# A seven-product form for the second MLP's output product, two blocks of tokens at a time

## The chip, the cores and the metric

The kernel runs on one NeuronCore of one Trainium2 chip. The metric is the device time of one execution in microseconds. Five engines have their own instruction queues: TensorE (PE in the profile; its weight loads are PEld), VectorE (DVE), ScalarE (ACT), GpSimd (POOL) and SyncE (SP), which here issues all DMAs.

## The reference, cut to what matters

```
attn = local attention over chunks of 32 tokens, with 8 memory slots   # 4 x 8 heads x 768 x 64
x = attn as 3072 tokens x 512
h = max(x @ w1, x @ w2, x @ w3)          # d_ff 768
y = h @ w_mid                            # 3072 x 512 (called moe_w_out)
u = y @ w_in                             # 512 -> 2048
g = u if u >= 1;  0 if u <= -1;  (u + 1)**2 / 4 between
out = g @ w_out                          # 2048 -> 512
```

The weights are float64 in memory, q, k, v and the memory float32, and so is the output.

## The kernel before, in words

Tokens are worked on in 6 blocks of 512 (`TB`), features in tiles of 128 (`P`). Every product is made of float32 operands that are split in a rounded high part (`hi`, type fp32r) and the rest (`lo`); `mm3` (L495) then issues three matmuls: hi x hi, hi x lo, lo x hi. A split is a ScalarE copy that writes `hi` and a subtraction on GpSimd or VectorE that writes `lo`.

Three stages follow one another. Up to about 450 us, the attention of later blocks runs interleaved with the first MLP (`slot_l1`, `slot_l2`) of earlier blocks; the order is a list written out by hand (`PLAN`, for block 0), and then a loop over `order` with one attention step for each slot. In its gaps the float64 weights of the second MLP are rounded (`round_step`: `abs_w`, `tail_w`, `bits_w`, `sum_w`), first 8 pairs of w_out tiles and then 8 pairs of w_in tiles, one pair in six slots, and stored to DRAM: w_out to `wd`, w_in to `cd` together with four sums of its quarters (`combine_w`). Then comes the first MLP of the last block, some 63 us, in which `LAST_BLOCK` names what else is done at each slot: the blocks' y is loaded and its sums made (`prep`), and w_out comes back from `wd` and is split (`w_step`, `split_w`).

From about 519 us the second MLP runs for three pairs of blocks. Its product with w_in is in the seven-product form already: the two halves of d_model and the two blocks of a pair are the quarters of one matrix, w_in's quarters those of the other. `pair_slot` (L662) makes the seven products of one n (eight n for a pair), adds them from the PSUM banks to the four result tiles (VectorE, L679 to L712) and applies the activation (`g_relu` on ScalarE, `g_rest` on VectorE). Between its products `mid` puts the product with w_out of the pair's first block (`slot_l4`, L724); the second block's runs after the pair's last n, 14 or 16 steps in a row. `slot_l4` is the ordinary product: for each of 16 tiles f of d_ff, four groups of 128 tokens, three matmuls each with 128 tokens of h stationary and 512 columns of w_out moving. For each f of a block, h is split once (`split`, ScalarE L513 and GpSimd L515). `split_c` splits a 256-wide w_in operand for a coming product (ScalarE L585, GpSimd L586). `NEXT_PAIR` names the steps at which `prep` of the next pair runs: loads of y's quarters A to D, differences T1 to T4 (L636, L639), and seven splits (L616, L617).

Each engine works through its queue in the order in which the program issues. A buffer tag with a number of `bufs` is a ring: a new tile of the tag waits until the oldest one's readers are done.

Of the kernel before, what the change touches and what calls it, by code (L numbers as in the profile page):

```python
# [65 lines left out]
def attention_then_two_mlps(ctx, tc, q, k, v, mem_k, mem_v, w1, w2, w3, w_mid, w_in, w_out, out):  # L66
# [38 lines left out]
    round2 = [("d", f) for f in range(K2)] + [("c", f + h) for f in range(HF) for h in (0, HF)]  # L105
# [45 lines left out]

    def combine_w(st, c):
# [33 lines left out]

    def load_w(q):
        n = 2 * (q - Q1)
        staged[q] = stage.tile([P, 2, TB], F32, tag="st", name=f"w{q}", bufs=2)
        nc.sync.dma_start(out=staged[q], in_=wd[n:n + 2].rearrange("t p f -> p t f"))  # L190

    def split_w(q, pool):
        new_w(q, pool)
        t = staged.pop(q)
        hi, lo = split2.pop(q)
        nc.scalar.copy(out=hi, in_=t)
        nc.vector.tensor_tensor(out=lo, in0=t, in1=hi.bitcast(F32), op=ALU.subtract)

# [344 lines left out]
    def slot_l2(j, f):  # L543
        hi, lo = hs.pop(("A", j, f))
        whi, wlo = weights["b", f]
        for d in range(KD):
            c = slice(d * P, (d + 1) * P)
            mm3(acc[d], whi[:, c], wlo[:, c], hi, lo, f == 0, f == K1 - 1)
            if f == K1 - 1:
                y = mx.tile([P, TB], F32, tag=("hh", "hl")[d % 2], name=f"y_{j}_{d}", bufs=3)  # L550
# [7 lines left out]
    OPERANDS = "b11 b21 b22 t1 t2 t3 t4".split()  # L558
    PRODUCTS = [(0, "b11"), (2, "t2"), (1, "b21"), (3, "t3"), (4, "t1"), (5, "t4"), (6, "b22")]
    PARTS = 4  # L560
    mat, raw, cs, late, keep = {}, {}, {}, {}, []
    total = NB // 2 * HF * 7
    put, loaded, limit = [0], [0], [HF * 7]

# [13 lines left out]
    def split_c():  # L578
# [5 lines left out]
        cs[s] = c = rp.tile([P, 2, HK], F32R, tag="cr", name=f"cs{s}", bufs=8)  # L584
# [22 lines left out]
    def halves_of(y):  # L607
        return [y[:, i] for i in range(2)] if not isinstance(y, list) else y

    def split_y(name, y):  # L610
        if name not in mat:
            mat[name] = new_mat(name)
        t = mat[name]
        for hi, lo, x in zip(halves_of(t[:, 0]), halves_of(t[:, 1]), halves_of(y)) if isinstance(y, list) else (
                (t[:, 0], t[:, 1], y),):
# [3 lines left out]
    def prep(p):  # L619

        v = {}

        def load(name, j, h):
            v[name] = y = stage.tile([P, 2, TB], F32, tag="c", name=f"{name}_{p}", bufs=2)
            nc.sync.dma_start(
                out=y, in_=yd[2 * h * P:2 * (h + 1) * P, j * TB:(j + 1) * TB].rearrange("(k p) t -> p k t", p=P))

        def load2(name, j, h):
            v[name] = [rp.tile([P, TB], F32, tag="cr", name=f"{name}{i}_{p}", bufs=8) for i in range(2)]
            for i in range(2):  # L630
                r = (2 * h + i) * P
                nc.sync.dma_start(out=v[name][i], in_=yd[r:r + P, j * TB:(j + 1) * TB])

        def sub(out, a, b):
            if not isinstance(v[a], list) and not isinstance(v[b], list):
                nc.vector.tensor_tensor(out=v[out], in0=v[a], in1=v[b], op=ALU.subtract)  # L636
                return
            for o, x, y in zip(*[halves_of(v[n]) for n in (out, a, b)]):
                nc.vector.tensor_tensor(out=o, in0=x, in1=y, op=ALU.subtract)  # L639

        return {
            "A": lambda: load("A", 2 * p, 0), "C": lambda: load("C", 2 * p + 1, 1),
            "B": lambda: load2("B", 2 * p + 1, 0), "D": lambda: load2("D", 2 * p, 1),
            "b11": lambda: split_y("b11", v["A"]), "b22": lambda: split_y("b22", v["C"]),
            "b21": lambda: split_y("b21", v["D"]),
            "T1": lambda: sub("B", "B", "A"), "T2": lambda: sub("C", "C", "B"),
            "T3": lambda: sub("A", "C", "A"), "T4": lambda: sub("D", "D", "C"),
            "t1": lambda: split_y("t1", v["B"]), "t2": lambda: split_y("t2", v["C"]),
            "t3": lambda: split_y("t3", v["A"]), "t4": lambda: split_y("t4", v["D"]),
        }  # L650

    def g_relu(x, a):
# [3 lines left out]
    def g_rest(x, a):  # L656
        nc.vector.scalar_tensor_tensor(out=a, in0=a, scalar=1.0, in1=x, op0=ALU.min, op1=ALU.max)

    def kept_h(f):
        return keep[f // 2][:, f % 2]  # L660

    def pair_slot(p, n, mid):  # L662

        s, j = (p * HF + n) * 7, 2 * p
        V = nc.vector
        add = partial(V.tensor_tensor, op=ALU.add)

        def next_product(k):
            bank = banks[4 + (s + k) % 4]
# [4 lines left out]
        c11 = mx.tile([P, TB], F32, tag="y", name=f"c11_{s}", bufs=2)  # L674
        nc.scalar.copy(out=c11, in_=b)
        split_c()
        b = next_product(1)
        c12 = mx.tile([P, TB], F32, tag="y", name=f"c12_{s}", bufs=2)
        add(out=c12, in0=b, in1=c11)  # L679
        split_c()  # L680
        mid(0)
        b = next_product(2)
        add(out=c11, in0=b, in1=c11)  # L683
        a11 = mx.tile([P, TB], F32, tag="t", name=f"a11_{s}", bufs=2)
        g_relu(c11, a11)
# [12 lines left out]
        split(("B", j, n), a11, f"b{j}_{n}")
        split_c()
        mid(1)  # L700
        g_rest(c22, h22)
        b = next_product(5)
        add(out=c21, in0=b, in1=c21)
        a21 = mx.tile([P, TB], F32, tag="t", name=f"a21_{s}", bufs=2)
        g_relu(c21, a21)
        split_c()
        if n == HF - 1:
            g_rest(c21, a21)
            split(("B", j, n + HF), a21, f"b{j}_{n + HF}")
            mid(2)  # L710
        b = next_product(6)
        add(out=c12, in0=b, in1=c12)  # L712
        h12 = kept_h(n)
        g_relu(c12, h12)
        if n < HF - 1:
            g_rest(c21, a21)
            split(("B", j, n + HF), a21, f"b{j}_{n + HF}")
            split_c()
            mid(2)
        else:  # L720
            split_c()
        g_rest(c12, h12)

    def slot_l4(i, f):  # L724
        hi, lo = hs.pop(("B", i, f))
        whi, wlo = weights["d", f]
        first, last = f == 0, f == K2 - 1
        for t in range(TB // P):
            c = slice(t * P, (t + 1) * P)
# [257 lines left out]
```

## Time and profile before

| | us |
|---|---|
| three runs | 1023.65, 1025.57, 1026.11 |
| median | 1025.57 |
| the profiled execution | 1025.52 |
| its span, first to last instruction | 1023.7 |

The profile is of one execution. Busy time of an engine is the time in which at least one of its instructions runs; a matmul's duration includes its way through the pipeline, so durations of neighbours overlap. The page and the answers give times in us from the start of the span, unless marked ns.

### The profile page before, as it was taken

The page shows a single profiled execution, that of the slowest core. Times are in us where ns is not written, and L with a number is a line of the kernel's source. Part 1 is how long each engine was busy: PE and PEld are TensorE (multiplying, and loading weights), DVE is VectorE, ACT ScalarE, POOL GpSimd, SP SyncE. Part 2 cuts the span into 40 slices and gives each one's busy share as a digit, 9 for nine tenths or more (in the row PEclk, how much of TensorE's full clock was granted, in tenths as well). Part 3 has the DMA queues.
Part 4 walks back from the last instruction along what each step waited for, and adds up shares of the span by engine and source line. Part 5 has one row for each costly group of instructions (what it writes and reads, how often), then busy time and mean ns, then how long its engine had stood idle before and what let it go on. Part 6 is the DMA issues. An engine that isn't in the chain of part 4 may idle for free.

```text
span 1023.7 us, 18842 instructions
## 1 busy us (share of the span) xinstructions
PE 1001.3 (98%) x7398; PEld 807.6 (79%) x7398; DVE 560.5 (55%) x880; ACT 473.7 (46%) x835; POOL 331.5 (32%) x316
## 2 busy tenths in 40 slices
PE   8899889999999999999999999999999999999998
PEld 6667678887787787788888888888888888888886
DVE  4689935456657766645365444465544384444410
ACT  6576434333224224224366554456555455555421
POOL 0024311111111111111345553575454366554343
PEclk9999999999999999999999999999999999999999
DMA  7767535555655666334322211313212302221011
GB/s 171 202 160 206 144 111 157 140 154 144 141 149 134 179 162 190 115 126 161 118 77 72 68 57 36 124 36 101 71 52 63 133 1 97 75 72 52 1 42 42
DMA packets 175305, 110.95 MB, mean 108 GB/s; under 512 B 127344, under 2 KB 147824, under 8 KB 175216
## 3 DMA queue, kind: packets, MB, share of 16 engines
q1 hardware_dynamic: 175216, 109.75, 37.6%
q8 instruction: 58, 0.95, 0.4%
q14 instruction: 31, 0.25, 0.1%
HBM read 85.59 MB, written 24.12 MB: 107 GB/s over the span
## 4 chain that ended last, share of the span: by engine, by line
PE 88%; DVE 8%; DMA 2%; issue 1%; ACT 1%; SPq 0%; POOL 0%; DVEq 0%; POOLq 0%; ACTq 0%
PE bank L496 20%; PE bank L497 19%; PE bank L498 19%; PE bank L730 9%; PE bank L731 9%; PE bank L732 9%; DVE c L144 2%; DVE c L141 1%; PE bank L409 1%; PE bank L367 1%; DVE c L149 1%; DMA kq<-in_k_dram 1%; DVE c L142 1%; PE bank L429 1%; DMA st<-in_moe_w_dram 1%
## 5 line engine op out<-in xcount | busy, mean ns | idle before, releaser
L496 PE MATMUL bank<-xh,hi 128*128 128x512 f32 x432 | 175.3, 406 | 1.2 <-ACT xh L437 0.7
L498 PE MATMUL bank<-xh,lo 128*128 128x512 f32 x432 | 169.2, 392 | 1.9 <-POOL lo L185 1.9
L497 PE MATMUL bank<-xl,hi 128*128 128x512 f32 x432 | 169.5, 392 | 0.3 <-DVE xl L441 0.2
L515 POOL TENSOR_TENSOR hl_a<-t,hh_a 128x512 fp32r<-128x512 f32 x34 | 47.3, 1391 | 342.3 <-ACT hh_a L513 286.2
L730 PE MATMUL bank<-hi,hh_b 128*128 128x512 f32 x384 | 149.9, 390 | 0.0
L731 PE MATMUL bank<-lo,hh_b 128*128 128x512 f32 x384 | 149.9, 390 | 0.0
L732 PE MATMUL bank<-hi,hl_b 128*128 128x512 f32 x384 | 149.4, 389 | 0.0
L498 PEld LDWEIGHTS bank<-xh,lo 128*128 128x128 f32 x432 | 81.4, 188 | 20.4 <-POOL lo L185 2.7
L496 PEld LDWEIGHTS bank<-xh,hi 128*128 128x128 f32 x432 | 81.5, 189 | 19.3 <-DVE t L531 1.0
L497 PEld LDWEIGHTS bank<-xl,hi 128*128 128x128 f32 x432 | 81.6, 189 | 16.0 <-DVE xl L441 1.0
L531 DVE TENSOR_TENSOR t<-bank,t 128x512 f32<-128x512 f32 x72 | 49.6, 688 | 81.3 <-PE bank L498 81.0
L586 POOL TENSOR_TENSOR cs<-ra,cs 128x256 fp32r<-128x256 f32 x96 | 73.5, 787 | 63.1 <-ACT cs L585 63.1
L515 POOL TENSOR_TENSOR hl_b<-a,hh_b 128x512 fp32r<-128x512 f32 x48 | 62.7, 1307 | 79.6 <-ACT hh_b L513 56.1
L730 PEld LDWEIGHTS bank<-hi,hh_b 128*128 128x128 f32 x384 | 72.1, 188 | 15.9
L732 PEld LDWEIGHTS bank<-hi,hl_b 128*128 128x128 f32 x384 | 72.1, 188 | 15.5
L515 POOL TENSOR_TENSOR hl_b<-h,hh_b 128x512 fp32r<-128x512 f32 x48 | 66.9, 1399 | 53.7 <-ACT hh_b L513 53.7
L731 PEld LDWEIGHTS bank<-lo,hh_b 128*128 128x128 f32 x384 | 72.1, 188 | 15.2
L653 ACT ACTIVATE a<-c 128x512 f32<-128x512 f32 x48 | 30.4, 633 | 103.2 <-DVE c L683 55.7
L497 PE MATMUL bank<-t,cs 128*128 128x512 f32 x192 | 76.1, 396 | 0.0
L498 PE MATMUL bank<-t,cs 128*128 128x512 f32 x192 | 76.0, 396 | 0.0
L496 PE MATMUL bank<-t,cs 128*128 128x512 f32 x192 | 76.0, 396 | 0.0
L586 POOL TENSOR_TENSOR cs<-rb,cs 128x256 fp32r<-128x256 f32 x72 | 57.8, 806 | 42.4 <-ACT cs L585 42.4
(134 smaller groups left out, 1845.4 us busy)
## 6 DMA issues: line engine op xcount, KB each, us to landing
ra<-cd SPq DMA_DIRECT2D x24, 512.0 KB
st<-in_moe_w_out_dram SPq DMA_DIRECT2D x22, 512.0 KB
st<-in_moe_w_dram SPq DMA_DIRECT2D x18, 512.0 KB
vw<-in_v_dram SPq DMA_DIRECT2D x152, 56.0 KB
st<-in_moe_w_in_dram SPq DMA_DIRECT2D x16, 512.0 KB
yd<-y SPq DMA_DIRECT2D x24, 256.0 KB
rb<-cd SPq DMA_DIRECT2D x24, 256.0 KB
out_dram<-ob SPq DMA_DIRECT2D x24, 256.0 KB
```

The source lines that it names most:

```text
L141: V.tensor_scalar(out=cf, in0=cf, scalar1=LEAST, scalar2=MOST, op0=ALU.max, op1=ALU.min)
L144: V.scalar_tensor_tensor(out=c, in0=staged[q][:, :, :, 1], scalar=0xC0000000, in1=c, op0=ALU.bitwise_and, op1=ALU.bitwise_or)
L496: nc.tensor.matmul(out, whi, xhi, start=first, stop=False)
L497: nc.tensor.matmul(out, whi, xlo, start=False, stop=False)
L498: nc.tensor.matmul(out, wlo, xhi, start=False, stop=last)
L515: e.tensor_tensor(out=lo, in0=h, in1=hi.bitcast(F32), op=ALU.subtract)
L531: nc.vector.tensor_tensor(out=cur["t", j, f], in0=s, in1=cur["t", j, f], op=ALU.max)
L586: nc.gpsimd.tensor_tensor(out=c[:, 1], in0=t, in1=c[:, 0].bitcast(F32), op=ALU.subtract)
L653: nc.scalar.activation(out=a, in_=x, func=AF.Relu, bias=0.5, scale=0.5)
L730: nc.tensor.matmul(acc[t], hi[:, c], whi, start=first, stop=False)
L731: nc.tensor.matmul(acc[t], hi[:, c], wlo, start=False, stop=False)
L732: nc.tensor.matmul(acc[t], lo[:, c], whi, start=False, stop=last)
```

## The change

The product with w_out is brought in the seven-product form too, over the two blocks of a pair and the two halves of d_ff (1024 each) and of d_model (256 each). It no longer runs between the pair's w_in products but after all of them, as one loop `pair_l4` of 7 products x 8 steps. A step has four groups of 128 tokens with three matmuls each: 128 tokens of h stationary, 256 columns of w_out or of a sum of its quarters moving.

- The four quarters of h of a pair are kept whole (`hq`); `sum_h` forms sums of them in place for products 3 to 6 (VectorE, at steps `S..`; 1024 elements, or twice 512 for the quarters 2 and 3 where h21 takes part). `split_h` splits the h of step i + 4 while step i runs; the low part is made on GpSimd, in 13 of the 56 steps (`ON_V`) on VectorE. The halves lie in a ring of nine (`hb`), which the w_in operands share.
- Three of w_out's seven operands stay in SBUF (`rd`, `load_d`, `split_d`: loaded and split in the last block); four are stored split (`td`) and loaded for each pair over the operands of the w_in product (`load_t`, at steps `L..`).
- The rounding of a w_out pair now forms sums (`combine_d`) and splits them (`streamed_d`, a step of its own, "p"); the store ("out") is five DMAs and one slot later, for w_in's too.
- The results are added up over the products from 256-wide halves of the banks (`evict`), and stored in eight DMAs a pair.
- `pair_slot` has no `mid` products any more; `fill` splits a w_in operand or, at a pair's end, the first h. `prep` of the next pair is at steps 28 to 55.
- The warm-up matmuls on `eye` (fp32r) become bf16 ones like the others; the copies that make `eye` go.

```diff
-    wd = dram.tile([K2, P, TB], F32, name="wd")
+    rd = dram.tile([HF, P, 3, HK], F32, name="rd")
+    td = dram.tile([4, HF, P, 2, HK], F32, name="td")
...
+    def combine_d(st, c):
...
+        sub(out=d[:, 0], in0=b22, in1=b12)
+        sub(out=b12, in0=b12, in1=b11)
+        sub(out=d[:, 1], in0=b22, in1=b12)
+        sub(out=d[:, 2], in0=b21, in1=d[:, 1])
+    def streamed_d(c, d):
+        for i, x in (0, d[:, 0:2]), (2, c[:, :, HK:]):
+            hi = d[:, 3 + i:5 + i]
+            nc.scalar.copy(out=hi.bitcast(F32R), in_=x)
+            nc.gpsimd.tensor_tensor(out=x.bitcast(F32R), in0=x, in1=hi, op=ALU.subtract)
...
-    def pair_slot(p, n, mid):
+    def pair_slot(p, n, mid, fill):
...
         b = next_product(4)
+        add(out=h22, in0=b, in1=c21)
+        g_start(h22)
         add(out=c12, in0=b, in1=c12)
+        g_end()
+        fill()
...
+    FACTORS = [("h22", 2), ("h11", 0), ("h12", 1), ("h22", "b22", "b11"), ("h21", "t2", "b21"), ("h11", "t3", "t1"),
+               ("h12", "t4", "b22")]
+    LEAD, ON_V = 4, range(1, 38, 3)
+    def split_h(i):
+        if i < 7 * HF:
+            x = h_tile(FACTORS[i // HF][0], i % HF)
+            hi, lo = next_half(), next_half()
+            nc.scalar.copy(out=hi, in_=x)
+            e = nc.vector if i in ON_V else nc.gpsimd
+            e.tensor_tensor(out=lo, in0=x, in1=hi.bitcast(F32), op=ALU.subtract)
+            ready.append((hi, lo))
+    def sum_h(k, g):
+        (o, a, b), op = {3: (("h22", "h21", "h22"), ALU.add), 4: (("h21", "h11", "h21"), ALU.subtract),
+                         5: (("h11", "h22", "h11"), ALU.subtract), 6: (("h12", "h12", "h11"), ALU.subtract)}[k]
+        for x, y, z in both((o, g), (a, g), (b, g)):
+            nc.vector.tensor_tensor(out=x, in0=y, in1=z, op=op)
...
+    def pair_l4(p, steps):
+        for i in range(7 * HF):
+            k, f = divmod(i, HF)
+            if f == 0:
+                done = cur.get("l4")
+                cur["l4"] = acc4 = [next_bank() for _ in range(TB // P)]
+            hi, lo = ready.pop(0)
...
+            for t in range(TB // P):
+                c = slice(t * P, (t + 1) * P)
+                o = acc4[t][:, 0:HK]
+                nc.tensor.matmul(o, hi[:, c], w[:, 0], start=f == 0, stop=False)
+                nc.tensor.matmul(o, hi[:, c], w[:, 1], start=False, stop=False)
+                nc.tensor.matmul(o, lo[:, c], w[:, 0], start=False, stop=f == HF - 1)
+            split_h(i + LEAD)
+            if k and f < TB // P:
+                evict(p, k - 1, f, done[f])
...
-    def slot_l4(i, f):
...
-    BY_PART = "out", "", "in in", "a", "", "b"
+    BY_PART = "p", "out", "in in", "a", "", "b"
...
+        L4_STEPS = {0: "L30 L31 L40", 1: "L41 L50 L51 L60", 4: "S30", 6: "S31", 8: "S32", 10: "S33",
+                    12: "S40", 14: "S41", 16: "S42", 18: "S43", 20: "S50", 21: "S51", 23: "S52", 25: "S53",
+                    27: "S60", 28: "L61 A", 29: "S61 B", 30: "D", 31: "S62", 32: "C", 33: "S63", 35: "b11", 36: "T1", 37: "T2",
+                    39: "t2", 41: "b21", 42: "T3", 44: "T4", 45: "t3", 49: "t1", 52: "c", 53: "t4 c", 54: "c", 55: "c c b22"}
```

`c` is `split_c`; the other names of `L4_STEPS` are steps of `prep` for the next pair, and nothing in the last one.

## Rows read from the trace of the kernel before

**Rows 1.** The page, busy time, share of the span and instructions by engine.

```profile
PE 1001.3 (98%) x7398; PEld 807.6 (79%) x7398; DVE 560.5 (55%) x880; ACT 473.7 (46%) x835; POOL 331.5 (32%) x316
```

**Rows 2.** The page, chain that ended last, by engine.

```profile
PE 88%; DVE 8%; DMA 2%; issue 1%; ACT 1%; SPq 0%; POOL 0%; DVEq 0%; POOLq 0%; ACTq 0%
```

**Rows 3.** Windows: stretch, length, busy (instructions) by engine, clock, DMA share, GB/s.

```profile
190.00:345.00 155.00, 155.00 (x1665) 123.91 (x1665) 96.22 (x184) 52.80 (x79) 16.58 (x12) 1.00 0.56 145
345.00:440.00 95.00, 95.00 (x1032) 75.92 (x1031) 64.06 (x121) 28.79 (x43) 10.11 (x7) 1.00 0.52 151
...
475.00:538.00 63.00, 63.00 (x278) 51.77 (x277) 35.46 (x43) 30.98 (x56) 22.86 (x22) 1.00 0.28 95
538.00:700.00 162.00, 162.00 (x705) 132.07 (x704) 83.01 (x107) 88.56 (x174) 86.35 (x88) 1.00 0.21 65
```

**Rows 4.** Grouped instructions by line, TensorE, the whole span.

```profile
L730 PE MATMUL bank<-hi,hh_b 128*128 128x512 f32 x384 | 149.9, 390 | 0.0
```

**Rows 5.** Timeline of TensorE, w_out alone: first and last of 55 matmuls.

```profile
659.62 0.39 PE L732 MATMUL bank<-hi,hl_b 128*128 128x512 f32 x1
...
671.86 0.39 PE L732 MATMUL bank<-hi,hl_b 128*128 128x512 f32 x1
```

**Rows 6.** Timelines of TensorE and its loads in the warm-up, cut at several times.

```profile
6.25 0.91 PE L833 MATMUL bank<-eye 128*128 128x256 f32 x5
...
6.46 0.70 PE L833 MATMUL bank<-eye 128*128 128x256 f32 x4
...
6.65 0.51 PE L833 MATMUL bank<-eye 128*128 128x256 f32 x3
...
7.00 0.27 PE L263 MATMUL bank<-ident,kq 128*128 128x128 f32 x1
...
6.77 0.19 PEld L833 LDWEIGHTS bank<-eye 128*128 128x128 f32 x1
```

**Rows 7.** Grouped instructions of ACT, DVE and POOL (L158: 350 to 475 us; others: 475 to the end).

```profile
L513 ACT CAST hh_b<-h 128x512 fp32r<-128x512 f32 x48 | 29.8, 620 | 60.8 <-PE bank L731 58.5 <-POOL hl_b L515 2.3
L654 ACT ACTIVATE a<-a 128x512 f32<-128x512 f32 x48 | 30.4, 633 | 1.5
L585 ACT CAST cs<-ra 128x256 fp32r<-128x256 f32 x96 | 34.0, 402 | 1.4 <-DMA ra<-cd 1.4
L586 POOL TENSOR_TENSOR cs<-ra,cs 128x256 fp32r<-128x256 f32 x96 | 73.5, 787 | 63.1 <-ACT cs L585 63.1
L657 DVE SCALAR_TENSOR_TENSOR h<-h,c 128x512 f32<-128x512 f32 x48 | 35.0, 728 | 23.1 <-ACT h L654 22.8
L679 DVE TENSOR_TENSOR c<-bank,c 128x512 f32<-128x512 f32 x24 | 16.6, 691 | 65.4 <-PE bank L498 64.8 <-ACT c L675 0.6
...
L158 DVE TENSOR_TENSOR st<-c 128x256 f32<-128x256 f32 x6 | 2.6, 425 | 0.2
```

**Rows 8.** Timelines of GpSimd and VectorE where the next pair is prepared.

```profile
655.81 1.29 POOL L515 TENSOR_TENSOR hl_b<-h,hh_b 128x512 fp32r<-128x512 f32 x1 [1.43 <-ACT hh_b L513]
658.52 1.42 POOL L515 TENSOR_TENSOR hl_b<-h,hh_b 128x512 fp32r<-128x512 f32 x1 [1.42 <-ACT hh_b L513]
661.26 1.53 POOL L515 TENSOR_TENSOR hl_b<-h,hh_b 128x512 fp32r<-128x512 f32 x1 [1.31 <-ACT hh_b L513]
...
656.72 1.47 DVE L617 TENSOR_TENSOR b<-A,b 128x1024 fp32r<-128x1024 f32 x1 [9.56 <-ACT b L616]
658.11 2.38 DVE L639 TENSOR_TENSOR B<-B,A 128x512 f32<-128x512 f32 x2
660.41 1.21 DVE L617 TENSOR_TENSOR b<-C,b 128x1024 fp32r<-128x1024 f32 x1
...
675.27 2.92 DVE L617 TENSOR_TENSOR t<-D,t 128x512 fp32r<-128x512 f32 x2
```

**Rows 9.** Waits of SP's queue: line, waited for, us in total, times, longest.

```profile
SPq L120 <- DMA cd<-st: 4.2, 2, 3.7
```

**Rows 10.** One tile's instructions: ns, shortest, median, longest.

```profile
L639 DVE TENSOR_TENSOR B<-B,A x6: 679/682/1781, 473.3 to 824.7; 128x512 f32<-128x512 f32 x6
```

**Rows 11.** Window with the y loads of the next pair, columns as in rows 3.

```profile
640.00:650.00 10.00, 10.00 (x46) 8.24 (x45) 2.77 (x4) 4.52 (x8) 4.80 (x4) 1.00 0.69 238
```

More of the change, by code (lines that the diff above doesn't have):

```diff
@@ L556, in slot_l2, with next_bank, next_half, h_tile @@
                     stores.append(store)
-    OPERANDS = "b11 b21 b22 t1 t2 t3 t4".split()
     PRODUCTS = [(0, "b11"), (2, "t2"), (1, "b21"), (3, "t3"), (4, "t1"), (5, "t4"), (6, "b22")]
     PARTS = 4
-    mat, raw, cs, late, keep = {}, {}, {}, {}, []
+    mat, raw, cs, late = {}, {}, {}, {}
+    hq, hb, fb, resident, ready = {}, [], [], {}, []
     total = NB // 2 * HF * 7
     put, loaded, limit = [0], [0], [HF * 7]
+    turn = {"bank": KD, "act": 0}
+    def next_bank():
+        turn["bank"] += 1
+        return banks[(turn["bank"] - 1) % 8]
+    def next_half():
+        assert len(cs) + 2 * len(ready) < len(hb)
+        hb.append(hb.pop(0))
+        return hb[-1]
+    def h_tile(q, n):
+        t = hq[q, n // 2]
+        return t[n % 2] if isinstance(t, list) else t[:, n % 2]
+    def both(*keys):
+        if any(isinstance(hq[k], list) for k in keys):
+            return [[h_tile(q, 2 * g + i) for q, g in keys] for i in range(2)]
+        return [[hq[k] for k in keys]]
     def load_c(g):
@@ L605, in new_mat @@
         return pool.tile([P, 2, 2, TB], F32R, tag=tag, name=name, bufs=2)
[L607 to L615, printed above, removed]
+    SPOT = {"A": ("h22", 0), "B": ("h22", 1), "D": ("h22", 2), "C": ("h22", 3), "E": ("h21", 0)}
@@ new lines, in attention_then_two_mlps @@
+    outs = []
+    def pair_l4(p, steps):
[5 more added lines that the diff above has]
+            hi, lo = ready.pop(0)
+            if k < 3:
+                w = resident[FACTORS[k][1], f // 2][:, f % 2]
+            else:
+                w = chunk_of(k, f)[:, f % 4]
+            for t in range(TB // P):
[7 more added lines that the diff above has]
+                evict(p, k - 1, f, done[f])
+            for name in steps.get(i, "").split():
+                if name[0] == "S":
+                    sum_h(int(name[1]), int(name[2]))
+                elif name[0] == "L":
+                    load_t(int(name[1]), int(name[2]))
+                elif name == "c":
+                    split_c()
+                elif p + 1 < NB // 2:
+                    prep(p + 1, name)
+        for t in range(TB // P):
+            evict(p, 6, t, cur["l4"][t])
+        del cur["l4"]
@@ L819, in mem_t @@
                         in_=tm[e * 64:e * 64 + 64, :, :, 2 * h + e, :])
-        eye = mx.tile([P, TB], F32R, tag="hl", name="eye", bufs=3)
-        for i in range(TB // P):
-            nc.scalar.copy(out=eye[:, i * P:(i + 1) * P], in_=ident)
-        warmed = [0]
         def warm(i):
-            warmed[0] += 1
-            b = eye if warmed[0] in (6, 7) else ident.bitcast(mybir.dt.bfloat16)
+            b = ident.bitcast(mybir.dt.bfloat16)
             t = banks[i]
             for _ in range(4):
-                nc.tensor.matmul(t[:, 0:2 * P], b[:, 0:P], b[:, 0:2 * P], start=True, stop=True)
+                nc.tensor.matmul(t[:, 0:2 * P], b[:, 0:P], b, start=True, stop=True)
         parts.update({
@@ L908, in attention_then_two_mlps @@
             l1_split(*x)
[L909 to L938 removed]
+        prep(0, "t1")
```

339 lines of the change are left out of this document (175 added, 164 removed).

## The prediction

> **What bounds the kernel now.** I read the page's busy shares first [rows 1]: TensorE is busy 98% of the span, no other engine above 55%. The chain of waits, which goes back from the last instruction to what released each, says the same: 88% of it is TensorE [rows 2]. The windows show where the other 12% are not: from 190 us on TensorE is busy for the whole of each stretch [rows 3]. So after the start the time is the number of matmuls times their spacing, and other engines count only where they come too late for the next one. The grouped lines give the numbers: L730 has 384 matmuls of 512 columns [rows 4], L731 and L732 as many, 1152 for w_out. Their 390 ns is a duration with the pipeline in it, not a price; the price is the distance from start to start. In a stretch that holds only w_out [rows 5] the first and the 55th start are 12.24 us apart: 12.24 / 54 = 0.227 us. So w_out costs 1152 x 0.227 = 261.5 us of the 1025.5 us of the profiled execution (span 1023.7 and some 1.8 us around it; the median of the runs, 1025.57, is the same to 0.1 us). All sums below are against 1025.5. What a measurement of this kernel can tell from no change is about 0.3%, 3 us.
>
> **The matmuls of the new form.** Seven products of 8 steps replace 8 block products: 56 steps a pair, 12 matmuls each, 3 pairs: 2016 matmuls, of 256 columns. In columns that is 7/8 of before, but there are 864 more instructions and as many more weight loads, so the spacing of a 256-column matmul decides. The trace has eight of them, in the warm-up on `eye` [rows 6]. The first stand 0.21 us apart, and from the start at 6.65 us the spacing is about half: three spacings take 7.00 - 6.65 = 0.35 us, 0.117 us each. [...] A weight load beside them lasts 0.19 us, yet three matmuls, each with a load of its own, begin within 0.35 us: loads overlap, and no matmul is held back by the whole of one. Low end: half of 0.227, 0.1135 us. [...] I take 0.117, the only direct row: 2016 x 0.117 = 235.9 us, **25.6 us less** than 261.5 (ends: 32.7 and 15.6 less).
>
> [...]
>
> **What must be ready for them.** A step of the new loop takes 12 x 0.117 = 1.40 us; a step of before took 12 x 0.227 = 2.72. Each step needs one split of a 128x512 tile into high and low part: ScalarE copies (0.62 us [rows 7]), then GpSimd subtracts (1.29 us undisturbed, the first GpSimd row of [rows 8]), or VectorE where the step is in `ON_V` (13 of 56). Half the time for the same split: that is where the change can lose. And VectorE and GpSimd hold each other up [rows 8]. VectorE's 1024-element subtraction of 656.72 ends 1.09 us after GpSimd's of 655.81 does; the pair of 512-element ones ends 0.55 after GpSimd's of 658.52; and GpSimd's of 661.26 ends 1.17 after VectorE's of 660.41. So operations with both inputs in SBUF run one after the other, at 1.17 us for a GpSimd split, 0.55 for a VectorE operation of 512 elements and 1.09 for one of 1024. Check: VectorE has no gap from 656.72 to 678.19, and in it are 5 of 1024, 12 of 512, 7 GpSimd splits and 2 halves at about 0.6: 5.5 + 6.6 + 8.2 + 1.2 = 21.5 us, the time it took. VectorE operations that read a bank do not take part: L679, the additions of the w_in products, stay at 0.69 us [rows 7].
>
> Now the shared path for one pair, product by product, against the 8 x 1.40 = 11.2 us of TensorE. Product 0: 5 GpSimd splits, 3 VectorE splits, 2 sums of 1024 (`S`): 5.9 + 1.7 + 2.2 = 9.7. Product 1: 5, 3, 2 sums of 1024 and 2 as two halves: 5.9 + 1.7 + 2.2 + 2.2 = 11.9. Product 2: 6, 2, 2 halved sums and 3 of 1024: 7.0 + 1.1 + 2.2 + 3.3 = 13.6. Product 3: 5, 3, 4 sums: 11.9. Product 4: 7, 1, 1 sum, and of the next pair's preparation T1, T2 and two splits of 1024: 8.2 + 0.6 + 1.1 + 4.4 = 14.2. Product 5: 8 splits, 4 of preparation: 13.7. Product 6: 4 splits, 2 of preparation, 5 splits of w_in at 0.79 at most: 10.8. The excess over 11.2 adds up to 0.7 + 2.4 + 0.7 + 3.0 + 2.5 = 9.3 us by the end of product 5. A step's low half can be written only when the step four before has left its buffer (the ring of 9 halves), and is first read by that step's third matmul: 3 x 1.40 + 0.2 - 1.29 = 3.1 us can be late unseen. So TensorE stands still 9.3 - 3.1 = 6.2 us in each of the first two pairs. The third prepares nothing: 3.8 - 3.1 = 0.7. Together **13.1 us back**. [...]
>
> **The rest.** The w_in products now stand alone: 42 x 0.23 = 9.7 us for one n. ScalarE has 9 operations of 0.63 and 7 of 0.40, 8.5 us, VectorE 7 of 0.69 and 4 of 0.73, 7.8, GpSimd 7 of 0.79, 5.5 [rows 7]. All fit; with 7 products of w_in halves split ahead I take no stall, but ScalarE enters the w_out loop some 2 to 3 us behind, which costs perhaps 0.5 a pair: **1.5 us**. In the attention stage the eight w_out pairs get four subtractions of 0.43 us, two ScalarE copies and two GpSimd subtractions more, and five stores for one. The w_in pairs already do the four subtractions there, and the windows before and after 345 us (w_out pairs, then w_in pairs) have TensorE busy throughout, with VectorE at 62% and 67% [rows 3]: I cost them at nothing. If the cover failed, each of 8 periods would lose at most the 1.7 us of VectorE, 14 us. The store now leaves one step later, just ahead of the next fetch in SP's queue; behind that stand the attention loads. SP's wait for such a store is 4.2 us in two cases today [rows 9], and no wait of TensorE's follows. In the last block the splits of `split_w` leave VectorE and 12 splits of 1.29 come to GpSimd: 15 us more in 63 of which 23 are busy [rows 3]. The warm-up and the tail (a 256-element addition for a 512-element copy) are worth under 0.5 us.
>
> Sum: 1025.5 - 25.6 + 13.1 + 1.5 = 1014.5; I say **1014**.
>
> **Rivals.**
> *Only TensorE counts.* VectorE's preparation slips to where GpSimd is idle, and lateness never exceeds 3.1 us. For it: nothing needs T1 to t4 before the next pair. Against it: VectorE gets its turn after each GpSimd operation [rows 8], needed or not. 1025.5 - 25.6 = 1000, down to 993 at 0.1135. Chance 0.14.
>
> *The path between VectorE and GpSimd costs each operation its whole undisturbed time* (1.29 for a GpSimd split, 0.68 for 512 elements on VectorE as L639's shortest [rows 10], 1.21 for 1024 as at 660.41 [rows 8]): the slower side. The products then need 10.9, 13.7, 15.5, 13.4, 15.8, 15.2 us: 17.5 us of excess, 8.9 in the last pair; less 3.1 each, 14.4 + 14.4 + 5.8 = 34.6: 1025.5 - 25.6 + 34.6 = 1034.5. It decides from an excess of some 11.6 us a pair on. VectorE waiting in order for ScalarE's copies can have the same effect. Against it: those prices give 24.8 us where 21.5 were measured. Chance 0.17.
>
> [...]
>
> *Transfers late.* L60 and before are 7 MB, at the 238 GB/s that a full queue shows [rows 11] 31 us, in time. Then b22's second chunk waits for step 27 and A, B, D, C follow: 3.1 MB, 13 us, step 37, and T2 is issued at 37. At half that rate T2 is 13 us late, VectorE and then ScalarE's copy for t2 stand, and TensorE stops from step 44: about 7 us a pair twice, 1028. Chance 0.08.
>
> *Loads bind.* A 256-column matmul costs its weight load's 0.188 us: 2016 x 0.188 = 379, 1143. The spacing in [rows 6] speaks against it: 0.02.
>
> **Numbers.** The forecast case, 1006 to 1021, has the remaining 0.59. Below 1022.5: 0.14, most of the forecast: 0.69 faster. Within 3 us: the forecast's upper tail and the late transfers, 0.13. Slower: 0.18. The range for 8 in 10, 1001 to 1034, takes in most of the first rival and half of the second; the forecast's own is 1006 to 1021.
>
> **What would show it.** Spacing in the new loop where nothing waits: 0.117, else the first term is wrong. TensorE waiting for GpSimd's low halves in products 2 to 5 of the first two pairs, 5 to 7 us each, hardly in the third; GpSimd without gaps there. No waits in the attention stage and the w_in stage; a wait there, or waits for ScalarE's halves or for `td`, would make the prediction wrong.

## The result and the profile after

The changed kernel takes 1034.57 us (median of 5 runs, 1032.38 to 1036.67), the kernel before 1025.28 in the same rounds: a ratio of 1.0099, interval 1.0074 to 1.0124. It is slower by some 9 us, where 1014 was forecast.

The page of the changed kernel, the lines that answer to [rows 1, 2]: busy time by engine, and the chain that ended last.

```profile
PE 986.8 (96%) x8262; PEld 834.3 (81%) x8262; DVE 734.7 (71%) x1081; ACT 520.9 (50%) x926; POOL 484.4 (47%) x377
...
PE 73%; DVE 14%; issue 4%; POOL 3%; ACT 2%; SPq 2%; DMA 1%; DVEq 0%; POOLq 0%; ACTq 0%
```

TensorE is busy 14.5 us less and still the span is 9.1 us longer (1023.7 to 1032.8): it waits now. VectorE's busy time rose by 174 us, GpSimd's by 153, and VectorE went from 8% to 14% of the chain.

The windows of the changed kernel show where: three of the attention stage, then the three w_out loops. The columns are those of [rows 3].

```profile
250.00:300.00 50.00, 45.99 (x448) 36.30 (x455) 30.31 (x58) 13.54 (x21) 8.92 (x7) 0.93 0.67 179
300.00:350.00 50.00, 47.58 (x508) 38.18 (x509) 31.95 (x67) 18.19 (x28) 7.67 (x6) 0.97 0.67 176
350.00:460.00 110.00, 110.00 (x1163) 88.01 (x1162) 72.20 (x136) 33.39 (x50) 11.40 (x8) 1.00 0.48 134
608.60:697.70 89.10, 83.04 (x673) 80.76 (x672) 80.43 (x80) 45.62 (x79) 77.14 (x45) 1.00 0.39 137
776.10:866.60 90.50, 83.50 (x673) 80.82 (x672) 81.66 (x82) 46.65 (x80) 77.17 (x45) 1.00 0.38 134
944.00:1028.80 84.80, 81.41 (x673) 80.29 (x672) 65.66 (x76) 38.70 (x68) 66.31 (x42) 1.00 0.34 119
```

Two places are new. From 250 to 350 us, while the w_out pairs are rounded, TensorE is no longer busy throughout (46.0 and 47.6 of 50 us, against 155.00 of 155.00 in [rows 3]) and the granted clock falls below 1.00. And the three loops take 89.1 + 90.5 + 84.8 = 264.4 us, no less than the 261.5 of before, with VectorE and GpSimd nearly full in the first two.

By stages: the first w_in product starts at 527.1 us instead of 519.1 (+8.0); from there to the last matmul it is 501.7 instead of 500.3 (+1.4: +2.9 in w_out, -1.5 elsewhere); the tail is 0.3 shorter. Together 9.1.

**The w_out loops.** The timeline of TensorE, changed kernel, first loop: the first matmuls of products 0 and 1, and one of the stalls.

```profile
608.62 0.28 PE L814 MATMUL bank<-d,hb 128*128 128x256 f32 x1
...
620.07 0.28 PE L814 MATMUL bank<-d,hb 128*128 128x256 f32 x1
...
635.92 0.28 PE L815 MATMUL bank<-d,hb 128*128 128x256 f32 x1
637.40 0.39 PE L816 MATMUL bank<-d,hb 128*128 128x256 f32 x1 [1.20 <-DVE hb L742]
```

Product 0 has 96 matmuls and no wait: 11.45 / 96 = 0.119 us each. 2016 x 0.119 = 240.0, so 264.4 - 240.0 = 24.4 us of the three loops are stalls. The products' lengths place them. A product without a stall is 11.4 us long; of products 0 to 6, 2 and 3 are 12.9 and 12.8 in every pair (8.4 us of stalls over three pairs), products 5 and 6 are 14.9 and 14.0 in the first two pairs only (12.1 us), and product 0 is 12.9 and 13.4 in the second and third (3.4 us).

What each stall waits for is in the waits of TensorE, changed kernel, whole span: what waits, for what, us in total, times, longest.

```profile
PE bank L816 <- POOL hb L742: 9.5, 18, 1.2
...
PE bank L435 <- DVE xs L428: 8.2, 4, 4.0
...
PE bank L816 <- DVE hb L742: 6.7, 6, 1.2
```

L742 is the subtraction that makes the low half. Eighteen waits are for GpSimd (products 5 and 6, where the next pair is prepared, and the entrances, the first steps of the second and third loop) and six for VectorE: two in each pair, at steps 19 and 25, both in `ON_V`. The timelines of VectorE and GpSimd, changed kernel, cut at several times, show how the two engines take turns, and at the end what VectorE does before the split of step 19, for which TensorE waits until 637.40.

```profile
614.76 1.12 DVE L742 TENSOR_TENSOR hb<-h,hb 128x512 fp32r<-128x512 f32 x1 [0.59 <-ACT hb L740]
615.80 2.31 DVE L758 TENSOR_TENSOR h<-h,h 128x1024 f32<-128x1024 f32 x1
618.84 0.96 DVE L742 TENSOR_TENSOR hb<-h,hb 128x512 fp32r<-128x512 f32 x1 [0.74 <-PE bank L816]
619.72 2.31 DVE L758 TENSOR_TENSOR h<-h,h 128x1024 f32<-128x1024 f32 x1
621.96 1.78 DVE L758 TENSOR_TENSOR h<-h,h 128x512 f32<-128x512 f32 x1
623.66 1.79 DVE L758 TENSOR_TENSOR h<-h,h 128x512 f32<-128x512 f32 x1
625.38 1.77 DVE L742 TENSOR_TENSOR hb<-h,hb 128x512 fp32r<-128x512 f32 x1
...
631.10 4.56 DVE L758 TENSOR_TENSOR h<-h,h 128x1024 f32<-128x1024 f32 x2
635.58 1.76 DVE L742 TENSOR_TENSOR hb<-h,hb 128x512 fp32r<-128x512 f32 x1
...
613.70 14.62 POOL L742 TENSOR_TENSOR hb<-h,hb 128x512 fp32r<-128x512 f32 x8 [0.69 <-ACT hb L740]
```

Beside GpSimd's splits a sum of 1024 (L758) takes 2.31 us and a half of 512 takes 1.78, against 1.21 [rows 8] and 0.68 [rows 10] undisturbed, and GpSimd's eight splits take 1.83 each against 1.29. A step lasts 12 x 0.119 = 1.43. So a low half that is given to GpSimd takes longer than a step while VectorE has sums to do, and one given to VectorE comes behind whatever sums were issued ahead of it: that of step 19 starts at 635.58, behind two sums of 1024, and ends at 637.34.

**The attention stage.** A unit here is one pass of the attention step; its start is that of its first `xs` matmul (L435). From the first unit's start after 190 us to the last's it takes 262.7 us instead of 252.0; the first starts 2.8 us earlier than before, which leaves the 8.0. The waits between 190 and 470 us, changed kernel, columns as above:

```profile
DVE kw L351 <- DMA kq<-in_k_dram: 14.2, 3, 9.5
...
PE bank L435 <- DVE xs L428: 6.4, 2, 4.0
...
DVE kw L351 <- DMA qs<-in_q_dram: 5.6, 1, 5.6
```

VectorE waits for loads of k and q, then TensorE for the VectorE result that comes out late (`xs`, 4.01 us at 274.71 and 2.42 at 337.87). In the kernel before VectorE's longest wait for such a load is 4.8 us and TensorE has none for `xs`. The timeline of SP's queue, changed kernel, shows why the loads are late.

```profile
244.87 0.52 SPq L846 DMA_DIRECT2D td<-st  x1
245.48 0.71 SPq L847 DMA_DIRECT2D td<-st  x1
246.28 1.16 SPq L848 DMA_DIRECT2D td<-c  x1
247.49 1.17 SPq L849 DMA_DIRECT2D rd<-c  x1
248.76 0.78 SPq L850 DMA_DIRECT2D rd<-st  x1
249.63 1.72 SPq L838 DMA_DIRECT2D kq<-in_k_dram  x3
252.64 0.83 SPq L119 DMA_DIRECT2D st<-in_moe_w_out_dram  x2
253.51 6.53 SPq L838 DMA_DIRECT2D kq<-in_k_dram  x9
...
263.82 3.84 SPq L838 DMA_DIRECT2D kq<-in_k_dram  x8
```

Five stores go first, then three k loads, then the fetch (L119), which overwrites `st` and has to wait until the stores have read it; nine k loads stand behind that fetch, and eight more further on. VectorE's wait of 9.5 us ends at 267.77, with those eight. They begin 12.6 us after the unit's start at 251.2; in the kernel before the first of them begin at 261.10, 7.1 us after a start at 254.0. The waits of SP's queue, changed kernel, 200 to 360 us:

```profile
SPq L846 <- ACT st L168: 5.2, 1, 5.2
...
SPq L119 <- DMA rd<-st: 3.0, 3, 1.4
SPq L121 <- DMA rd<-st: 2.5, 2, 2.1
```

The first is a store that waits for ScalarE's copy in `streamed_d`; it is issued at 305.45, ahead of the second stall. The others are the fetches (L119 of w_out, L121 of w_in) that wait for the last store's transfer, 1.2 us of it at 252.64. The windows around the first stall, changed kernel, show a second price.

```profile
266.00:270.00 4.00, 4.00 (x79) 3.10 (x78) 2.23 (x5) 0.86 (x1) 0.00 (x0) 1.00 0.53 141
270.00:274.00 4.00, 0.71 (x4) 0.24 (x2) 3.86 (x9) 0.00 (x0) 0.00 (x0) 0.90 0.90 271
274.00:278.00 4.00, 3.29 (x10) 2.81 (x11) 2.17 (x4) 1.10 (x2) 0.95 (x1) 0.50 0.60 198
```

After 4 us with hardly a matmul the granted clock is 0.50, and the nine matmuls of 512 columns from 276.06 to 279.47 begin 0.426 us apart, against 0.229 from 268.03 to 270.32. Cut every 5 us it is 0.82, 0.50 and 0.99 from 270 to 285, and after the second stall 0.81 and 0.85 from 335 to 345. The starts of the units show what each part costs: a unit lasts 19.4 us where nothing waits, and from 251.2 on they last 23.5, 21.9, 19.4, 21.9 and 21.0. That is 6.6 us in the two units in which TensorE waits and 4.1 in the two behind them, at the lower clock: together the 10.7. The lower clock is not needed for a loss: of the five executions two have a mean clock of 0.998 and 0.997 and still take 1033.72 and 1032.38 us, the others 0.993 and 0.994 and 1034.57 to 1036.67.

### The profile page after: what moved, and what is told of

It reads as the page before. It is cut to its first block, busy times and chain, and to the rows that moved or that the text cites. A ratio compares the mean times of both kernels' runs of the same rounds, so it can differ in the third digit from the quotient of the medians.

```text
span 1032.8 us, 21358 instructions
## 1 busy us (share of the span) xinstructions
PE 986.8 (96%) x8262; PEld 834.3 (81%) x8262; DVE 734.7 (71%) x1081; ACT 520.9 (50%) x926; POOL 484.4 (47%) x377
## 4 chain that ended last, share of the span: by engine, by line
PE 73%; DVE 14%; issue 4%; POOL 3%; ACT 2%; SPq 2%; DMA 1%; DVEq 0%; POOLq 0%; ACTq 0%
PE bank L502 18%; PE bank L503 18%; PE bank L504 18%; PE bank L816 5%; PE bank L815 5%; PE bank L814 5%; POOL hb L742 3%; DVE h L758 3%; DVE c L145 2%; DVE hb L742 2%; DVE c L142 2%; PE bank L373 1%; DVE c L150 1%; PE bank L415 1%; DVE c L143 1%
## 5 line engine op out<-in xcount | busy, mean ns | idle before, releaser
L742 POOL TENSOR_TENSOR hb<-h,hb 128x512 fp32r<-128x512 f32 x129 | 222.4, 1747 | 47.6 <-PE bank L816 24.8
L740 ACT CAST hb<-h 128x512 fp32r<-128x512 f32 x168 | 101.7, 619 | 101.1 <-PE bank L816 88.3
L616 POOL TENSOR_TENSOR hb<-ra,hb 128x256 fp32r<-128x256 f32 x96 | 89.0, 946 | 53.1 <-ACT hb L615 42.4
L502 PEld LDWEIGHTS bank<-xh,hi 128*128 128x128 f32 x432 | 82.3, 190 | 19.3 <-DVE t L537 1.0
L758 DVE TENSOR_TENSOR h<-h,h 128x1024 f32<-128x1024 f32 (+1 forms) x60 | 95.9, 1629 | 0.0
L678 ACT ACTIVATE f<-h 128x512 f32<-128x512 f32 x96 | 60.6, 631 | 57.3 <-DVE h L707 36.3
L816 PE MATMUL bank<-d,hb 128*128 128x256 f32 x288 | 82.1, 285 | 5.7 <-DVE hb L742 3.6
L685 DVE SCALAR_TENSOR_TENSOR h<-f,h 128x512 f32<-128x512 f32 x96 | 79.6, 829 | 8.5 <-ACT f L679 8.4
L814 PE MATMUL bank<-d,hb 128*128 128x256 f32 x288 | 81.4, 283 | 0.0
L815 PE MATMUL bank<-d,hb 128*128 128x256 f32 x288 | 81.3, 282 | 0.0
L502 PE MATMUL bank<-t,hb 128*128 128x512 f32 x192 | 75.5, 393 | 0.8 <-ACT h L560 0.8
L503 PE MATMUL bank<-t,hb 128*128 128x512 f32 x192 | 75.5, 393 | 0.0
L504 PE MATMUL bank<-t,hb 128*128 128x512 f32 x192 | 75.5, 393 | 0.0
L616 POOL TENSOR_TENSOR hb<-rb,hb 128x256 fp32r<-128x256 f32 x72 | 63.2, 889 | 21.9 <-ACT hb L615 20.1
L204 POOL TENSOR_TENSOR lo<-c,hi 128x1024 fp32r<-128x1024 f32 x10 | 25.0, 2502 | 99.0 <-ACT hi L199 99.0
```

The costliest lines, as they stand in the source:

```text
L502: nc.tensor.matmul(out, whi, xhi, start=first, stop=False)
L503: nc.tensor.matmul(out, whi, xlo, start=False, stop=False)
L504: nc.tensor.matmul(out, wlo, xhi, start=False, stop=last)
L616: nc.gpsimd.tensor_tensor(out=c[:, 1], in0=t, in1=c[:, 0].bitcast(F32), op=ALU.subtract)
L685: nc.vector.scalar_tensor_tensor(out=x, in0=a, scalar=1.0, in1=x, op0=ALU.min, op1=ALU.max)
L740: nc.scalar.copy(out=hi, in_=x)
```

## The experiments

Ratios are against the kernel before in the same rounds. Two questions were open, one for each place, and then whether both losses can be taken away together.

**What stalls the loops: the path between VectorE and GpSimd, or something else?** If it is the path, stalls go where operations are taken off it or moved to the engine that does them cheaper (0.68 us for VectorE's split at 613.49, 1.29 for GpSimd's at 638.88); if it is the operands' transfers or TensorE's own spacing, they stay.

*no_sums* leaves out the sums of h's quarters, so that products 3 to 6 work on other operands; all splits and matmuls are there.

```diff
                 if name[0] == "S":
-                    sum_h(int(name[1]), int(name[2]))
+                    pass
```

> The changed kernel without the sixteen sums of the quarters of h in each pair (products 3 to 6 then work on other operands). Theory 'path': 17 to 18 us of the shared path are gone for each pair; the stalls before step 34 vanish, those of the next pair's preparation (steps 42 to 54, about 6 us in the first two pairs) stay: total near 1021. Rival 'order', that only VectorE's lateness counts: the same for the first part, and the stalls from 42 on go as well, since VectorE is not late any more: near 1014.

Measured: 1021.33 us, ratio 0.9965 (0.9944 to 0.9987), 1.34% or 13.7 us under the changed kernel's ratio, as the theory 'path' expected. The loops take 84.5, 86.1 and 81.4 us, 12.4 less in all. The waits for VectorE at steps 19 and 25 are gone; of the 6.0 us a pair in products 5 and 6 of the first two pairs, where the next pair is prepared, 4.6 and 4.3 stay. So the sums make the one kind of stall, and GpSimd's turns beside the preparation most of the other.

*more_on_vector* gives 36 of the 56 low halves to VectorE instead of 13.

```diff
-    LEAD, ON_V = 4, range(1, 38, 3)
+    LEAD, ON_V = 4, [1] + [j for j in range(4, 56) if j % 8 not in (1, 4, 6) or j in (25, 41)]
```

> The changed kernel with 36 of the 56 low halves made on VectorE in place of 13 (5 to 6 of 8 in each product). Theory 'path': what is short is the path that VectorE's two-input operations and GpSimd share; a split takes 0.55 us of it on VectorE and 1.17 on GpSimd, so the products need 10 to 11.2 us of it against TensorE's 11.4, and the stalls of the three pairs (9.1, 10.6, 4.8 us) fall to some 2 us each: total near 1015. Rival 'order': TensorE waits because VectorE works in order and comes late behind its sums; with more splits on VectorE it waits more, total above 1040.

Measured: 1016.09 us, ratio 0.9916 (0.9888 to 0.9943), again near what 'path' expected; the rival's 1040 is refuted. The attention stage is as in the changed kernel. Windows of this kernel, the three loops:

```profile
608.60:689.30 80.70, 80.25 (x673) 80.04 (x672) 77.57 (x102) 45.73 (x78) 38.47 (x25) 1.00 0.42 148
766.90:849.30 82.40, 81.04 (x673) 80.22 (x672) 79.15 (x104) 46.82 (x80) 38.61 (x25) 1.00 0.41 145
926.80:1008.80 82.00, 80.80 (x673) 80.15 (x671) 67.01 (x98) 38.71 (x68) 32.05 (x20) 1.00 0.36 123
```

The loops are down to 80.7 + 82.3 + 82.0 = 245.0 us. GpSimd's busy time (fifth engine column) halves, from 77.1 to 38.5, and VectorE's, which got 23 more splits a pair, falls from 80.4 to 77.6: its operations wait less for GpSimd's turns (the preparation's L651, of 1024 elements, lasts 1.21 us at 673.41 and at 676.85, and 1.95 on average in the changed kernel's first loop). Of the remaining 5 us most is at the entrance of the second and third pair, where the split of step 1 stands in VectorE's queue ahead of additions of the w_in product and waits 1.84 us for ScalarE at 765.51.

**What makes the k loads late?** The changed kernel has, in each rounding of a w_out pair, five stores for one, a later slot for them, 1.4 MB instead of 0.5 (eleven quarters of 128x256 f32 for four), more work on three engines, and stores that read `st`. Each was tried, by itself or with others, on the changed kernel or on the kernel before. What the added stores write into the kernel before is read by nothing.

*two_stores* keeps the changed kernel and its bytes, but lays the eleven quarters out in one tensor, so that a pair leaves in two DMAs; each load of `td` becomes two.

```diff
-                nc.sync.dma_start(out=td[0:4, f, :, 0, :].rearrange("m p c -> p m c"), in_=d[:, 3:7])
...
-                nc.sync.dma_start(out=rd[f][:, 2], in_=d[:, 2])
+                nc.sync.dma_start(out=dd[f][:, 0:7], in_=d[:, 0:7])
+                nc.sync.dma_start(out=dd[f][:, 7:11].rearrange("p m f -> p (m f)"), in_=c.rearrange("p i f -> p (i f)"))
```

> The changed kernel with the same 1.4 MB of each w_out pair stored by two DMAs in place of five (a tile-shaped layout in DRAM; the later loads of the products 3 to 6 take two DMAs each). Theory 'issue': in the attention stage the changed kernel is late because SP has to issue five stores for one, about 0.5 us each, in front of the k and q loads; with three issues fewer the waits of VectorE's transposes for the k loads (9.5 and 5.6 us) fall to near those of the kernel before (4.8 and 2.3), and the last attention unit comes 6 to 10 us earlier: total near 1026. Rival 'bytes': the 0.9 MB more of each pair, or the added work on VectorE and GpSimd, is what delays; then the attention stage stays as in the changed kernel, total within 2 us of 1034.6.

Measured: 1029.60 us, ratio 1.0045 (1.0024 to 1.0065): 0.54% or 5.5 us better than five stores. VectorE's longest wait for k is 7.3 us, TensorE's for `xs` 2.9 in all, the granted clock is 1.00 in every 5 us from 240 to 380, and its last unit starts at 448.4 instead of 455.8. The loops stay (264.0). That lies between the two theories: fewer DMAs help, but the waits do not fall to those of the kernel before. The trace is of an execution of 1027.67 us, the third fastest of ten (1024.02 to 1034.25); two of the slower ones have a mean clock of 0.995, so the lower clock does occur in this kernel too.

*before_small_stores* (four more stores of 4 KB) asks for the issues alone, *before_late_store* for the slot, *before_big_store* (one more store of 1 MB) for the bytes.

```diff
+                for i in range(4):
+                    nc.sync.dma_start(out=xd[q - Q1, i], in_=c[:, 0, 8 * i:8 * i + 8])
```

> The kernel before with four more stores of 4 KB each behind the store of every rounded w_out pair (the data is not read again). Theory 'issue': four more issues by SP in a period of 19.4 us delay the k and q loads, and the attention stage gets 4 to 10 us longer: total 1030 to 1036. Rival 'bytes': 16 KB more for each pair is nothing, total within 2 us of 1025.3.

```diff
-    BY_PART = "out", "", "in in", "a", "", "b"
+    BY_PART = "", "out", "in in", "a", "", "b"
```

> The kernel before with the stores of rounded pairs one slot later, directly ahead of the next fetch in SP's queue, as in the changed kernel. Theory 'place': SP then waits for the store before it may fetch into its buffer, and the k and q loads behind come late; the attention stage gets 2 to 5 us longer, total near 1028. Rival: one slot is not seen, total within 1.5 us of 1025.

```diff
+                nc.sync.dma_start(out=xd[q - Q1].rearrange("o p f -> p o f"),
+                                  in_=c.rearrange("p (o i) f -> p o (i f)", o=1).to_broadcast([P, 2, 2 * TB]))
```

> The kernel before with one more store of 1 MB behind the store of every rounded w_out pair (its data twice, not read again): 1.5 MB for a pair, in two DMAs, against 1.4 MB in five in the changed kernel. Theory 'bytes': the transfers that are queued behind it, k and q among them, land some 4 to 5 us later, VectorE's transposes wait for them, and the attention stage gets 3 to 8 us longer: total 1028 to 1033. Rival 'neither': the stage stays, total within 1.5 us of 1025, and the cause is in the work of VectorE, ScalarE and GpSimd on the pair or in all of it together.

Measured: 1.0002 (0.9991 to 1.0013), 1.0001 (0.9987 to 1.0014) and 1.0002 (0.9989 to 1.0015). VectorE's longest wait for k is 4.3, 3.7 and 4.5 us. None of the three costs anything by itself.

*before_four_stores* adds issues and bytes together (four stores of 256 KB from `c`); *before_with_work* adds the work of `combine_d` and `streamed_d`, on data that nothing reads, with the later slot; *before_work_and_stores* is both.

```diff
+                for i in range(4):
+                    k = i % 2
+                    nc.sync.dma_start(out=xd[i, q - Q1], in_=c[:, :, k * HK:(k + 1) * HK])
```

> The kernel before with four more stores of 256 KB behind each rounded w_out pair, in pieces of 1 KB like those of the changed kernel (1.5 MB in five DMAs for a pair; the data is not read again). Theory 'stores': neither four issues nor 1 MB more delay anything alone, but together they do: the k loads are issued later and land behind more; the attention stage gets 4 to 8 us longer, total 1028 to 1031. Rival 'work': SP is late because the store waits for GpSimd's splits of the pair, or VectorE for its sums; then this stays within 1.5 us of the kernel before.

> The kernel before with the changed kernel's work on each w_out pair (four subtractions on VectorE, two copies on ScalarE, two subtractions on GpSimd; its results are not used) and its store one slot later, behind that work in SP's queue; one store of 512 KB as before. Theory 'stores': no delay, within 1.5 us of the kernel before. Rival 'work': the attention stage gets 4 to 8 us longer, total 1028 to 1031.

> Both additions to the kernel before: the work, the later slot, and four more stores of 256 KB. If either theory holds alone, this gives what that one gave. If only all of it together is too much for the slack of the k loads, this alone is 6 to 10 us longer, total 1030 to 1034, with VectorE's transposes waiting 7 to 10 us for a k load and TensorE for the normalized rows behind them.

Measured: 1.0006 (0.9991 to 1.0021), 1.0007 (0.9994 to 1.0019) and 1.0006 (0.9996 to 1.0016). The time expected of the two together was missed: neither these transfers nor the work nor both make the loss. VectorE's wait for k does grow with the stores, to 6.2 and 6.4 us, but TensorE waits 0.8 us at most.

*before_stores_from_st* differs from the last in the source of the four stores: they read `d`, which lies in `st`, where GpSimd has just worked and into which the next fetch writes (in pieces of 2 KB instead of 1).

```diff
-                    k = i % 2
-                    nc.sync.dma_start(out=xd[i, q - Q1], in_=c[:, :, k * HK:(k + 1) * HK])
+                    nc.sync.dma_start(out=xd[i, q - Q1], in_=d[:, 2 * i:2 * i + 2])
```

> As before_work_and_stores, but the four more stores read the tile into which the next fetch writes (the one that holds the sums), as three of the five do in the changed kernel, so that the fetch, and the k loads behind it in SP's queue, wait for the transfers to end. There VectorE waited 6.4 us for a k load, and TensorE lost 0.8. Theory 'slack': VectorE can wait for a k load some 5.5 us before TensorE notices, each part of the change adds 1 to 3 us, and only the sum goes over; here the wait comes to 8 to 9.5 us, TensorE loses 3 to 4 at that place and some more at half clock behind it: total 1028 to 1032. Rival: the tile's place makes no difference, within 1.5 us of before_work_and_stores, and what else is in the changed kernel's attention stage stays open.

Measured: 1036.81 us, ratio 1.0113 (1.0074 to 1.0153), beyond the 1028 to 1032 that were expected. Its waits between 190 and 470 us, first those of VectorE and TensorE, then SP's queue:

```profile
DVE kw L362 <- DMA kq<-in_k_dram: 16.1, 3, 10.2
...
PE bank L446 <- DVE xs L439: 8.3, 2, 4.6
DVE kw L362 <- DMA qs<-in_q_dram: 6.9, 1, 6.9
...
SPq L777 <- POOL st L167: 6.5, 1, 6.5
...
SPq L119 <- DMA xd<-st: 4.7, 4, 2.4
```

The same view of *before_work_and_stores*, whose stores read `c`:

```profile
DVE kw L362 <- DMA kq<-in_k_dram: 10.7, 3, 6.4
...
PE bank L446 <- DVE xs L439: 0.8, 1, 0.8
```

The last two lines of the first fence are what the second kernel does not have: SP's queue waits for GpSimd's split ahead of a store, and for the store's transfer ahead of the fetch. With them VectorE's wait goes from 6.4 to 10.2 us, TensorE's from 0.8 to 8.3, the granted clock is 0.50 from 275 to 280 and from 340 to 345 us, after each of the two stalls, and the last unit starts at 458.6 instead of 446.6. Place, size and the fall of the clock are those of the changed kernel's loss, in which SP's queue has the same two kinds of wait. Which of them weighs more was not separated by a run. The wait for the producer alone does not make the loss: in *two_stores*, whose first store reads `st` too, SP waits 5.3 us once for ScalarE's copy, and TensorE's waits for `xs` are down to 2.9. Of the waits for a store's transfer one of 3.0 us is left there, against five with 5.5 us in the changed kernel.

**Both losses away.** *vector_and_two_stores* joins *two_stores* with 34 low halves on VectorE; steps 1 and 50 stay with GpSimd.

```diff
-    LEAD, ON_V = 4, range(1, 38, 3)
+    LEAD, ON_V = 4, [j for j in range(4, 56) if j % 8 not in (1, 4, 6) and j != 50 or j in (25, 41)]
```

> The changed kernel with two DMAs for a pair's store and 34 of the 56 low halves on VectorE, none of the first four (the second one stood on VectorE ahead of the w_in additions and waited there 1.8 us for ScalarE) and not the one for step 50. If the two causes are apart, their gains add: 18.5 us of the path, 5 us of the stores and some 3 us of the waits that were left at the start of the w_out loops and at step 50: near 1009. If they are not, near 1016.

Measured: 1003.86 us, ratio 0.9818 (0.9789 to 0.9847): some 19 us under the kernel before and, by the ratios (1.0099 - 0.9818 = 2.81%), 29 under the changed one; 5 less than expected. Windows of this kernel, the three loops:

```profile
598.90:679.40 80.50, 80.39 (x674) 80.14 (x674) 76.10 (x100) 45.11 (x77) 37.70 (x25) 1.00 0.45 145
756.85:837.85 81.00, 80.88 (x674) 80.25 (x674) 78.52 (x101) 45.44 (x78) 41.97 (x27) 1.00 0.45 144
915.15:995.85 80.70, 80.69 (x673) 80.19 (x672) 65.87 (x94) 37.41 (x66) 35.33 (x22) 1.00 0.39 125
```

TensorE is busy throughout, the loops take 241.6 us against the 240.0 of the spacing alone, most of the entrances' stalls went with the split of step 1, and the attention stage's last unit starts at 446.1. Against the changed kernel that is 22.8 us in the loops and 9.7 up to the last unit's start (8.7 of it within the attention stage), 32.5 of the 33.0 between the two profiled spans. The profiled execution, at 1001.55 us, is the fastest of four.

*early_split* moves `streamed_d` right behind `combine_d` and the stores back to the first slot, so that they have more time before the fetch.

```diff
-    BY_PART = "p", "out", "in in", "a", "", "b"
+    BY_PART = "out", "", "in in", "a", "", "b p"
```

> The kernel of the run before it in this list, with a pair's split right behind its sums and the stores back at the slot they had in the kernel before. Theory 'place': the last 3 us of the attention stage's loss go, near 1006. Rival: ScalarE and GpSimd now stand in front of the pair earlier, VectorE's sums are waited for by ScalarE in its queue, and the time stays within 1.5 us of the run before or rises.

Measured: 1005.88 us, ratio 0.9833 (0.9812 to 0.9854), no better: VectorE's longest wait for k or q is 5.3 us instead of 5.6, TensorE's for `xs` 2.2 instead of 1.9. With two stores there was little left to win here.

## Why the prediction was wrong, point by point

The prediction's sum was 1014.5; the profiled execution is 1034.6 (span 1032.8 and 1.8 around it). The 20.1 us between them are 4.1 in the spacing, 9.8 in the stalls, 8.0 up to the first w_in product, and -1.8 elsewhere.

**The step that failed** is, first, the one about the attention stage: "I cost them at nothing", where the stage took 10.7 us more, and with it the sentence on SP's queue, that a wait of 4.2 us there is followed by no wait of TensorE's. I read that TensorE was busy throughout and that SP's waits were harmless, and took both for room. How much of it was used already stood in the trace of before, and I did not look: VectorE's own wait for the k loads, 4.8 us at its longest. Over the runs, that wait and what TensorE then waits for `xs` go together: 3.2, 4.8 and 6.2 us give 0; 6.4 gives 0.8; 7.3 gives 2.9; 9.2 gives 6.0; 9.5 gives 6.4; 10.2 gives 8.3; 10.4 gives 7.2. In the two kernels with both remedies 5.6 and 5.3 give 1.9 and 2.2, so the longest wait alone does not settle it; but in these runs the room ends somewhere between 4.8 and 6.4 us, and the kernel before already used 4.8. The bound that I gave for a failed cover (14 us) did hold the loss of 10.7, but I gave it no chance and no rival; and it was reckoned from VectorE's work, which *before_with_work* shows to cost nothing. Neither this step nor the next alone makes the miss: without the 8.0 us the time would be some 1026.6, without the 9.8 some 1024.8.

**The spacing** was 0.119 us, not 0.117: 4.1 us, inside the ends that I gave (32.7 and 15.6 us less are 0.1135 and 0.122). No run shows the 0.122: the granted clock is 1.00 in the kernel before from 5.40 to 7.00 us, where the matmuls on `eye` first stand 0.21 us apart, and the runs showed 0.119 where nothing waits.

**The stalls** were the other term that failed, by its size: 24.4 us where 13.1 + 1.5 were summed. Products 5 and 6 of the first two pairs, where the next pair is prepared, have 12.1 us of them, against 6.2 twice in the forecast, and those of the third none. The nearness is partly luck: by the forecast's excess TensorE would have stood 0.7 us in product 3, 3.0 in product 4, 2.5 in product 5 and not in product 6, where 0.1, 3.5 and 2.6 were measured in 4, 5 and 6. Missing were the 8.4 us at steps 19 and 25 in every pair: I added up the work on the shared path by product and let all of it be late together, but a split on VectorE is late on its own account, behind the sums issued ahead of it (two of 1024 at step 19), though the path as a whole is not behind (GpSimd itself waits 0.79 us for TensorE before its split of 633.12). At the entrances it was 3.4 instead of 1.5.

**The shared path's prices** held. Between the eight GpSimd splits of 613.70 to 628.32 VectorE gets seven turns, three splits, two sums of 1024 and two halves of 512: by my prices 8 x 1.17 + 5 x 0.55 + 2 x 1.09 = 14.3 us, by the whole undisturbed times 8 x 1.29 + 5 x 0.68 + 2 x 1.21 = 16.1, measured 14.62. So the rival with 1034.5 has the number of the result but not its cause: its price is refuted by this stretch, and 8.0 of the 20.1 us came from another stage.

**The other rivals.** Late transfers: no wait of TensorE's for `td` or its splits. Loads bind: the matmuls stand 0.119 us apart, not 0.188. *Only TensorE counts* gave 1000; it describes not this kernel but the one with both losses taken away, at 1003.86, whose loops take 241.6 us where next to nothing waits.

## What to carry to other kernels

That an engine is busy throughout says that its suppliers are in time, not by how much: before work or transfers are added to a stage, read how long the supplier itself already waits for its loads, and take that from the room. Look also at what a store from a tile into which the next fetch writes puts into the issuing engine's order: in *before_stores_from_st* SP's queue waited 6.5 us for such a store's producer and 4.7 for the stores' transfers ahead of the fetch, and VectorE's longest wait for the loads behind them was 10.2 us, against 6.4 in *before_work_and_stores*. And where two engines take turns on one path, count each operation against its own deadline in its engine's order, not only the path's total; moving 23 splits a pair to the engine that does them in half the time (0.68 us instead of 1.29) took 19.4 us off the three loops.

## What the runs showed of the hardware

- VectorE and GpSimd: moving 23 of 43 GpSimd subtractions a pair to VectorE lowered VectorE's busy time (80.4 to 77.6 us in the first loop). In the changed kernel a sum of 1024 beside GpSimd's splits took 2.31 us instead of 1.21, while the additions that read a bank took 0.41 us in both kernels. Eight turns of GpSimd and seven of VectorE took 14.62 us, where their whole undisturbed times make 16.1.
- Weight loads of 0.19 us each overlap: in product 0 of the changed kernel 96 matmuls of 256 columns, each with a load, followed at 0.119 us, and the first loop of *vector_and_two_stores* took 80.5 us for its 672, 0.120 each, with the loads' own column busy for 80.14 us. Whether the load or the matmul sets the 0.119 was not tried.
- In the changed kernel TensorE waited 4.01 us until 274.71; the granted clock was 0.50 from 274 to 278, and the unit behind the one with the wait lasted 21.9 us instead of 19.4. In *before_stores_from_st*, with 8.3 us in two such waits, it was 0.50 from 275 to 280 and from 340 to 345. In the profiled execution of *two_stores*, whose waits for `xs` are 1.8 and 1.1 us, it was 1.00 in every 5 us from 240 to 380.
